# Starting the loads of queries and keys from ScalarE's DMA queue instead of SyncE's, from step 28 on

## The chip, the core and the metric

The kernel runs on one core of a Trainium2 chip. A core has a matrix engine (TensorE, PE in the profile, with its weight loads as PEld), three engines for everything else (VectorE or DVE, ScalarE or ACT, GpSimd or POOL), and SyncE (SP), which here only starts transfers. Transfers between the chip's main memory and the core's on-chip memory are done by 16 DMA engines. An engine starts one by an instruction in its own queue; an instruction that has to wait for a semaphore holds everything behind it in that queue. The metric is device time in microseconds (us).

## The reference

There are 8 batches, 8 heads, 512 local positions, 32 global positions and a head width of 64. Attention comes first, then a two-layer network with a SiLU-like gate on its output.

```python
k_all = concat([k_g, k_l]); v_all = concat([v_g, v_l])
out_g = softmax(q_g @ k_all.T / 8) @ v_all                # 32 global queries see everything
s_ll  = where(|i - j| <= 32, q_l @ k_l.T / 8, -1e9)       # a local query sees a band
out_l = softmax(concat([q_l @ k_g.T / 8, s_ll])) @ v_all  # and the global keys
x = concat([out_g, out_l]) as rows of 8 heads x 64 = 512  # 4608 rows
h = x @ w_in                                              # 512 -> 2048
out = (h * sigmoid(h)) @ w_out                            # 2048 -> 512
```

## The kernel before

**Attention** is cut into 128 steps: 8 batches by 4 chunks of 128 positions by 4 pairs of heads. A step `k` is made of parts, each a small function: `st_load` fetches queries and keys of the step (tile `raw`), `st_split` cuts them into a high and a low half (a cast on ScalarE, L345, and two subtractions on VectorE, L346 and L347, into the tiles `qk` and `klo`), `st_scores` does the score matmuls (L363, L364) and the softmax, `st_halves`, `st_away` and `st_back` transpose the probabilities by a copy on GpSimd (L393), a write to main memory (L398) and a transposing load (L402, tile `pt`), and `st_out` multiplies by the values (L444) for the four pairs of a chunk at once. Steps 0 to 27 have a shorter form: their `raw` (L323) is used as it is, without a split.

The **global queries** of a batch come in four loads (`g_load`, tile `raw_g`, L238), each with its own split (`g_split`: L247 on ScalarE, L248 and L249 on VectorE) and scores (`g_scores`). Those of batches 0 and 1 (`GF` = 2) are not split. Those of batch `b + 1` are placed among the steps of batch `b`; for batches 2 to 7 that is at every second step from the eighth on, so those of batch 2 begin at step 23.

The **network** runs over 12 blocks of three (the last two: two) tiles of 128 rows. A block is 16 units; a unit `f` is a first layer (12 matmuls, L600), a gate (tanh L607 on ScalarE, L608 on VectorE, the high half `gh` L610 on ScalarE, the low half `gl` L611 on VectorE) and a second layer (9 matmuls, L627). TensorE does the second layer of a unit after the first layer of the next one, so the gate has that long. The attention of the next block is woven into the units of this one: `put(when, part, ...)` gives each part a due time in steps, the parts are sorted by it, and `fill` and `advance` emit them between the matmuls as the units proceed.

**What sets the order.** TensorE keeps the order in which the program emits its instructions. The other engines' order is made by a planner from its estimate of all times, except that `hold(...)` pins an instruction behind the instruction emitted just before it for the same engine. All transfers of SyncE's queue are held, so that queue has program order: loads, writes of halves, transposing loads and values. A transposing load waits for the write of its halves and for TensorE to release a `pt` tile (there are four); the write waits for GpSimd's copy.

**The due times around the change.** A step's load is due 1.65 steps before its scores (`DMAT`), its split 0.5 before them. `SOONER` makes the loads of steps 9 to 15 due earlier. A `raw_g` load is due 0.9 before the place of its scores' step, its split 0.2 after it. From step 16 on, and for the global queries from batch 2 on, `raw` and `raw_g` share two buffers: a load waits until the split of the load two places before has read its buffer.

ScalarE's queue starts only the stores of the results (L645).

Of the kernel before, what the change touches and what calls it, by code (L numbers as in the profile page):

```python
# [32 lines left out]
GW = QG + SKV  # L33
# [6 lines left out]
BUFS = dict(qk=2, raw=2, p=2, halves=1, pt=4)  # L40
ND = 28
KF = 12
GF = 2
KP = 12
WHOLE, OWN, SOONER = 9, 7, -2.2
WARM = 288
WARMS = (14, 8, 1)
LEAN = 8
# [23 lines left out]
def attention_moe_kernel(ctx: ExitStack, tc: tile.TileContext, qk0_in, qk_in, v_in, gqk, wts, out):  # L72
    nc = tc.nc
# [15 lines left out]
    def attbank(kind, name):  # L89
        if early:  # L90
            i = next(banks[kind]) % {"s": 3, "t": 2, "o": 3}[kind]
            if i and kind == "s":
                return ps_h.tile([P, 512], F32, tag="h", name=name)
            if i:
                return ps_out.tile([P, 512], F32, tag="out2" if kind == "t" else f"out{i - 1}", name=name)
        else:
            kind = "sto"[next(banks["s"]) % 3]
        return ps_att.tile([P, 512], F32, tag=f"att{kind}", name=name)


    hold = tc.keep_in_program_order
# [66 lines left out]
    def raw_tile(name, whole=False):  # L168
        i = next(homes) if whole else 0
        if i > WHOLE + NPR - 1:  # L170
            return const.tile([P, 2 * DM], F32, tag=f"ws{12 - (i - WHOLE - NPR) % 6}", name=name)
        if whole and i == NPR:
            return scratch(13, F32, name)
        i = (i - (i > NPR)) % 4
        if i % 2 and 14 + i // 2 not in taken:
            return scratch(14 + i // 2, F32, name)
        return raws.tile([P, QW + KW], F32, tag="raw", name=name)
# [57 lines left out]

    def g_load(b, p):
        raw = raw_tile(f"raw_g{b}_{p}", b < GF)
        hold(nc.sync.dma_start(out=raw[:, :GW], in_=gqk[b, p]))  # L238
        state["graw", p] = raw

    def g_split(b, p):
        if b < GF:
            return
        raw = state.pop(("graw", p))
        hi, lo = qk_tiles(f"_g{b}_{p}")

        nc.scalar.copy(out=hi[:, QG : QG + GW], in_=raw[:, :GW])  # L247
        nc.vector.tensor_tensor(out=lo, in0=raw[:, QG:GW], in1=hi[:, 2 * QG : QG + GW].bitcast(F32), op=ALU.subtract)  # L248
        nc.vector.tensor_tensor(out=hi[:, :QG], in0=raw[:, :QG], in1=hi[:, QG : 2 * QG].bitcast(F32), op=ALU.subtract)  # L249
        state["gqk", p] = hi, lo  # L250

    def g_scores(b, p):
        did(("scores", b, p), *([("turn", b - 1, p // 2)] if b else []))
        rows = slice(QG * (p % 2), QG * (p % 2 + 1))
        if b < GF:
            raw = state.pop(("graw", p))
        else:
            hi, lo = state.pop(("gqk", p))
            both, kh = hi[:, : 2 * QG], hi[:, 2 * QG : GW + QG]
        if b < GF:  # L260
            s = attbank("so"[p % 2], f"gs{b}_{p}")
# [58 lines left out]
    def st_load(k, b, c, pr):  # L320
        raw = raw_tile(f"raw{k}", k < WHOLE + OWN)
        if k < ND:
            hold(nc.sync.dma_start(out=raw[:, : QW + W], in_=qk0_in[k]))  # L323
        else:
            hold(nc.sync.dma_start(out=raw, in_=qk_in[k - ND]))
        tiles["raw", k] = raw

    def st_vload(k, b, c, pr):
# [20 lines left out]
    def st_scores(k, b, c, pr):  # L349
# [28 lines left out]
        else:  # L378
            nc.scalar.activation(p[:, 0, :W], p[:, 0, :W], AF.Copy, scale=st[:, 6:7])  # L379
        if KF <= k < ND:  # L380
            nc.scalar.activation(p[:, 1, :W], p[:, 1, :W], AF.Copy, scale=st[:, 7:8])
# [23 lines left out]
    def st_turn(k, b, c, pr):  # L405
        if k < KF:
            t = attbank("t", f"t{k}")
            p = tiles.pop(("p", k))
            assert k in held_by.values()
            for i in range(4):  # L410
                nc.tensor.transpose(t[:, i * P : (i + 1) * P], p[:, i * P : (i + 1) * P], ident.bitcast(F32))
            pt = tiles["pt", k] = pt_tile(k)
            nc.scalar.copy(out=pt[:, :, :, :P], in_=t.rearrange("p (u a q) -> p u a q", u=2, a=2))
        else:
            pt = tiles["pt", k] = pt_tile(k)
        if k < NPR:
            return
        did(("last", b) if (c, pr) == (NC - 1, NPR - 1) else k, ("turn", b, pr // 2))
        pgt, pgu = state["pgt"]
        nc.gpsimd.tensor_copy(out=pt[:, :, 0, P:], in_=pgt[:, c, 2 * pr : 2 * pr + 2, :])  # L420
        if c == NC - 1:
            src = pgu[SG * pr : SG * (pr + 1), :].rearrange("p (u q) -> p u q", u=2)
            nc.gpsimd.tensor_copy(out=pt[:SG, :, 1, P:], in_=src)
# [75 lines left out]
    def put(when, fn, *a):  # L499
        stream.append((when, fn, a))  # L500

    AHEAD = NPR
    for k, (t, b, c, pr) in enumerate(steps):
        a = (k, b, c, pr)
        j = k % NST
        due = dict(DUE)
        if k >= KF:
            due.update(DMAT)
            due.update({} if pr else DMAT0)
        if WHOLE <= k < WHOLE + OWN:  # L510
            due["load"] = SOONER
        if k < AHEAD:
            due.update({part: FIRST[part][k] - k for part in ("load", "vload", "turn", "out")})
        elif pr == 0:
            due["vload"] = VLOADS[min(k // NPR, 3)]
        if k == AHEAD:
            for h in range(NPR):
                put(FIRST["gload"][h], g_load, 0, h)
                put(FIRST["gscores"][h], g_scores, 0, h)
            for hh in range(2):  # L520
                put(FIRST["gsoft"][hh], g_soft, 0, hh)
                put(FIRST["gturn"][hh], g_turn, 0, hh)
            put(FIRST["late"], g_late)
            at = FIRST["then"]
            for when in JOINS:
                put(at + when - NPR, join_weights)
            for f, when in enumerate(SPLITS):
                put(at + when - NPR, split_weights, f)
        if j == 0 and b:
            for hh in range(2):  # L530
                put(at + (TURN if b > 1 else TURN1)[hh], g_turn, b, hh)
        for f, half in FIRSTW.get(k, ()):
            put(at + 0.01, fetch_weights, f, half)
        put(at + due["load"], st_load, *a)
        put(at + due["split"], st_split, *a)
        put(at, st_scores, *a)
        if "vload" in due:
            put(at + due["vload"], st_vload, *a)
        if k >= KF:
            put(at + due["halves"], st_halves, *a)  # L540
            put(at + due["away"], st_away, *a)
        put(at + due["turn"], st_turn, *a)
        if k >= KF:
            put(at + due["back"], st_back, *a)
        if k < SINGLE or pr == NPR - 1:
            n = 1 if k < SINGLE else NPR
            put(at + due["out"], st_out, k - n + 1, n, b, c, t)
            marks[t] = at + due["out"]
        if j == NST - 1 and b % 4 == 3:
            put(marks[t] + 0.001, g_tile, t + 1)  # L550
            marks[t + 1] = marks[t] + 0.001
        if b + 1 < B:
            first, every = HEADS if b > 1 else HEADS0
            for h in [h for h in range(NPR) if first + h * every == j]:
                for part, fn in (("load", g_load), ("split", g_split), ("scores", g_scores)):
                    put(at + (SOONER if part == "load" and b + 1 < GF else HEAD[part]), fn, b + 1, h)
                if h % 2:
                    put(at + HEAD["soft"], g_soft, b + 1, h // 2)
                at += HEAD["slot"]
        at += 1.0  # L560
# [178 lines left out]
```

## Time and profile before

| | |
|---|---|
| time, median of 3 runs | 980.89 us (979.16 to 983.91) |
| the profiled execution | 978.29 us, span 976.5 us |
| TensorE busy | 949.8 us, 97% of the span |
| ScalarE busy | 580.5 us, 59% |
| VectorE busy | 626.5 us, 64% |
| loads `raw<-in_qk_dram` with a split | 100, of 352 KB, 3.4 us from issue to landing |
| loads `raw_g<-in_gqk_dram` | 32 (24 of them from batch 2 on), of 304 KB, 4.6 us |
| transposing loads `pt<-away` | 116, 3.3 us |

A row of the profile names a line of the kernel, the engine, the operation and `out<-in`. In a list of time, the first number is the start in us from the span's beginning and the second the duration; what stands in brackets is how long the engine had been idle before, and what ended it. `SPq` and `ACTq` are the queues in which SyncE and ScalarE start transfers; the time of such a row is that of starting it, not of the transfer. In a list of waits the three numbers are the sum in us, the count and the longest. The chain that ended last is followed back from the last instruction, each time to what released it.

### The profile page before, as it was taken

The page shows a single profiled execution, that of the slowest core. Times are in us where ns is not written, and L with a number is a line of the kernel's source. Part 1 is how long each engine was busy: PE and PEld are TensorE (multiplying, and loading weights), DVE is VectorE, ACT ScalarE, POOL GpSimd, SP SyncE. Part 2 cuts the span into 40 slices and gives each one's busy share as a digit, 9 for nine tenths or more (in the row PEclk, how much of TensorE's full clock was granted, in tenths as well). Part 3 has the DMA queues.
Part 4 walks back from the last instruction along what each step waited for, and adds up shares of the span by engine and source line. Part 5 has one row for each costly group of instructions (what it writes and reads, how often), then busy time and mean ns, then how long its engine had stood idle before and what let it go on. Part 6 is the DMA issues. An engine that isn't in the chain of part 4 may idle for free.

```text
span 976.5 us, 17412 instructions
## 1 busy us (share of the span) xinstructions
PE 949.8 (97%) x5774; PEld 848.3 (87%) x5774; DVE 626.5 (64%) x1893; ACT 580.5 (59%) x1486; POOL 201.4 (21%) x413
## 2 busy tenths in 40 slices
PE   8789999999999999999999999999999999999998
PEld 6579888998899989989899999989989899899897
DVE  5888977766666677656577567766677565453322
ACT  6878876665556656555566656666575665343332
POOL 2122232122221222112122222312222221120000
PEclk9999999999999999999999999999999999999999
DMA  9968967576565766534655676566665664433000
GB/s 302 392 194 210 280 160 205 151 168 173 147 167 155 198 153 179 166 93 110 187 158 159 147 213 173 144 193 153 167 186 152 161 163 141 121 90 87 1 22 22
DMA packets 189305, 157.32 MB, mean 161 GB/s; under 512 B 128672, under 2 KB 148640, under 8 KB 189216
## 3 DMA queue, kind: packets, MB, share of 16 engines
q1 hardware_dynamic: 184800, 148.28, 56.2%
q10 hardware_dynamic: 4416, 7.93, 2.3%
q8 instruction: 46, 0.75, 0.3%
q14 instruction: 43, 0.35, 0.1%
HBM read 86.44 MB, written 39.32 MB: 129 GB/s over the span
## 4 chain that ended last, share of the span: by engine, by line
PE 82%; ACT 6%; DVE 6%; DMA 4%; issue 1%; SPq 0%; ACTq 0%; POOL 0%; DVEq 0%
PE out L627 34%; PE h L600 34%; PE o L444 6%; DMA raw<-in_qk_dram 2%; PE s L363 2%; PE s L364 2%; DMA raw_g<-in_gqk_dram 2%; ACT probs L372 1%; PE s L361 1%; DVE w_lo L231 1%; DVE w L221 1%; PE gt L309 1%; DVE probs L368 1%; DVE gl L611 1%; PE gs L272 0%
## 5 line engine op out<-in xcount | busy, mean ns | idle before, releaser
L393 POOL COPY halves<-probs 128x512 uint16<-128x512 uint16 x232 | 152.7, 684 | 495.2 <-ACT probs L379 185.2
L607 ACT ACTIVATE t<-h 128x384 f32<-128x384 f32 (+1 forms) x192 | 90.6, 472 | 166.5 <-PE h L600 156.3
L608 DVE SCALAR_TENSOR_TENSOR t<-t,h 128x384 f32<-128x384 f32 (+1 forms) x192 | 101.6, 529 | 115.1 <-ACT t L607 114.3
L627 PE MATMUL out<-w_hi,gh 128*128 128x512 f32 x544 | 164.9, 402 | 3.0 <-ACT gh L610 2.9
L600 PE MATMUL h<-xh,w_hi 128*128 128x384 f32 (+1 forms) x768 | 161.1, 332 | 4.6 <-ACT w_hi L230 4.5
L627 PE MATMUL out<-w_hi,gl 128*128 128x512 f32 x544 | 162.0, 396 | 0.2 <-DVE gl L611 0.2
L627 PE MATMUL out<-w_lo,gh 128*128 128x512 f32 x544 | 161.7, 395 | 0.0
L600 PE MATMUL h<-xh,w_lo 128*128 128x384 f32 (+1 forms) x768 | 158.8, 328 | 0.1
L600 PE MATMUL h<-xl,w_hi 128*128 128x384 f32 (+1 forms) x768 | 158.8, 328 | 0.0
L372 ACT ACTIVATE probs<-probs,st 128x224 f32<-128x224 f32 x244 | 115.8, 475 | 60.4 <-DVE st L368 59.7
L600 PEld LDWEIGHTS h<-xh,w_hi 128*128 128x128 f32 x768 | 133.7, 189 | 19.8 <-ACT w_hi L230 6.3
L611 DVE TENSOR_TENSOR gl<-t,gh 128x384 fp32r<-128x384 f32 (+1 forms) x192 | 109.6, 571 | 43.5 <-ACT gh L610 39.1
L368 DVE CUSTOM_DVE_ANT_0 probs<-s,mask 128x224 f32<-128x224 f32 x244 | 85.8, 386 | 75.6 <-PE s L364 64.8
L600 PEld LDWEIGHTS h<-xl,w_hi 128*128 128x128 f32 x768 | 133.4, 189 | 0.0
L600 PEld LDWEIGHTS h<-xh,w_lo 128*128 128x128 f32 x768 | 131.8, 189 | 0.7 <-DVE w_lo L231 0.7
L610 ACT CAST gh<-t 128x384 fp32r<-128x384 f32 (+1 forms) x192 | 94.4, 492 | 53.5 <-DVE t L608 52.9
L627 PEld LDWEIGHTS out<-w_hi,gl 128*128 128x128 f32 x544 | 100.7, 189 | 23.1 <-DVE gl L611 1.3
L627 PEld LDWEIGHTS out<-w_lo,gh 128*128 128x128 f32 x544 | 100.7, 188 | 21.7 <-issue 0.6
L627 PEld LDWEIGHTS out<-w_hi,gh 128*128 128x128 f32 x544 | 93.6, 189 | 15.7 <-ACT gh L610 6.5
L345 ACT CAST qk<-raw 128x704 fp32r<-128x704 f32 x100 | 77.7, 777 | 28.3 <-DMA raw<-in_qk_dram 23.8
L346 DVE TENSOR_TENSOR klo<-raw,qk 128x448 fp32r<-128x448 f32 x100 | 65.3, 653 | 30.4 <-ACT qk L345 28.1
L379 ACT ACTIVATE probs<-probs,st 128x224 f32<-128x224 f32 x118 | 56.7, 481 | 32.4 <-DVE st L375 30.8
(95 smaller groups left out, 1066.0 us busy)
## 6 DMA issues: line engine op xcount, KB each, us to landing
raw<-in_qk_dram SPq DMA_DIRECT2D x100, 352.0 KB, 3.4
away<-halves SPq DMA_DIRECT2D x116, 256.0 KB, 2.7
vraw<-in_v_dram SPq DMA_DIRECT2D x30, 512.0 KB, 4.9
raw_w<-in_wts_dram SPq DMA_DIRECT2D x29, 512.0 KB, 6.7
raw_g<-in_gqk_dram SPq DMA_DIRECT2D x32, 304.0 KB, 4.6
out_dram<-o ACTq DMA_DIRECT2D x29, 256.0 KB, 3.6
raw<-in_qk_dram SPq DMA_DIRECT2D x28, 240.0 KB, 4.8
pt<-away SPq DMA_TRANSPOSE x116, 3.3
```

Source lines behind the costliest of these rows:

```text
L345: nc.scalar.copy(out=qk, in_=raw)
L346: nc.vector.tensor_tensor(out=klo[:, :KW], in0=raw[:, QW:], in1=qk[:, QW:].bitcast(F32), op=ALU.subtract)
L368: nc.vector.tensor_tensor_reduce(out=p[:, u, :W], in0=ss[u], in1=mask_of[c], scale=-SCALE, scalar=3.0e38, op0=ALU.add, op1=ALU.min, accum_ ...
L372: nc.scalar.activation(p[:, u, :W], p[:, u, :W], AF.Exp, bias=st[:, u : u + 1], scale=-1.0, accum_out=st[:, 2 + u : 3 + u])
L393: nc.gpsimd.tensor_copy(out=halves[:, :, u], in_=p[:, 2 * P * u : 2 * P * (u + 1)].bitcast(U16).rearrange("p (j h) -> p h j", h=2))
L444: nc.tensor.matmul(o[D * u : D * (u + 1), :m], vraw[:, a, u, :], pt[:, u, a, :m], start=(a == 0), stop=(a == 1))
L600: nc.tensor.matmul(h[:, :nt], wt[:, c * P : (c + 1) * P], x[:, c, :nt], start=(i == 0), stop=(i == 3 * NCC - 1))
L607: nc.scalar.activation(t[:, :nt], h[:, :nt], AF.Tanh, scale=0.5)
L608: nc.vector.scalar_tensor_tensor(out=t[:, :nt], in0=t[:, :nt], scalar=1.0, in1=h[:, :nt], op0=ALU.add, op1=ALU.mult)
L610: nc.scalar.copy(out=gh[:, :nt], in_=t[:, :nt])
L611: nc.vector.tensor_tensor(out=gl[:, :nt], in0=t[:, :nt], in1=gh[:, :nt].bitcast(F32), op=ALU.subtract)
L627: nc.tensor.matmul(outs[n][i], g[:, i * P : (i + 1) * P], w, start=(f == 0 and j == 0), stop=(f == NF - 1 and j == 2))
```

## The change

The loads of queries and keys from step 28 on (`OTHER`), which are the 100 loads with a split, and the 24 loads of global queries from batch 2 on are started from ScalarE's queue instead of SyncE's. They are still held, now behind the instruction that the program emitted just before for ScalarE. The due time of the step loads becomes 1.4 steps before the scores (`LATER`) instead of 1.65; that of the global loads stays.

```diff
 KF = 12
+OTHER = 28
 GF = 2
 KP = 12
-WHOLE, OWN, SOONER = 9, 7, -2.2
+WHOLE, OWN, SOONER, LATER = 9, 7, -2.2, -1.4
...
     def g_load(b, p):
         raw = raw_tile(f"raw_g{b}_{p}", b < GF)
-        hold(nc.sync.dma_start(out=raw[:, :GW], in_=gqk[b, p]))
+        hold((nc.scalar if b >= GF else nc.sync).dma_start(out=raw[:, :GW], in_=gqk[b, p]))
...
         else:
-            hold(nc.sync.dma_start(out=raw, in_=qk_in[k - ND]))
+            hold((nc.scalar if k >= OTHER else nc.sync).dma_start(out=raw, in_=qk_in[k - ND]))
...
             due.update(DMAT)
             due.update({} if pr else DMAT0)
+        if k >= OTHER:
+            due["load"] = LATER
```

## The prediction

> **What bounds the kernel now.** I read the page first, then the stretches of 25 us, then the chain that ended last, then SyncE's queue.
>
> ```profile
> span 976.5 us, 17412 instructions
> PE 949.8 (97%) x5774; PEld 848.3 (87%) x5774; DVE 626.5 (64%) x1893; ACT 580.5 (59%) x1486; POOL 201.4 (21%) x413
> ```
>
> TensorE is busy for 97% of the span, and its order and its work are the same after the change. So the change can only move what TensorE loses by waiting or by a lower clock. The change acts from step 23 (the first moved load of global queries) and step 28 on, which is from about 141 us. Where TensorE is not full after that:
>
> ```profile
> 150.00:875.00 725.00, 718.87 (x4333) 648.93 (x4333) 476.47 (x1426) 427.97 (x1081) 164.23 (x324) 1.00 0.60 158
> ```
> ```profile
> 150.00:175.00 25.00, 24.42 (x151) 21.77 (x151) 20.26 (x57) 16.46 (x41) 6.06 (x12) 1.00 0.66 186
> ...
> 225.00:250.00 25.00, 23.51 (x145) 21.24 (x145) 14.37 (x43) 13.61 (x34) 4.92 (x9) 1.00 0.70 195
> 250.00:275.00 25.00, 22.67 (x118) 20.17 (x115) 17.54 (x55) 15.58 (x40) 5.48 (x12) 0.93 0.59 160
> ...
> 350.00:375.00 25.00, 24.73 (x153) 22.07 (x152) 19.46 (x59) 16.41 (x41) 5.38 (x13) 1.00 0.73 182
> ...
> 450.00:475.00 25.00, 24.46 (x150) 21.83 (x148) 13.12 (x39) 11.60 (x30) 4.87 (x9) 1.00 0.43 121
> 475.00:500.00 25.00, 24.78 (x151) 22.06 (x152) 18.80 (x52) 16.66 (x40) 6.67 (x12) 1.00 0.62 164
> ...
> 625.00:650.00 25.00, 24.71 (x152) 22.04 (x151) 17.82 (x52) 15.71 (x40) 6.62 (x13) 1.00 0.59 172
> ...
> 825.00:850.00 25.00, 24.64 (x150) 21.93 (x150) 13.12 (x39) 11.67 (x30) 4.62 (x10) 1.00 0.39 103
> ```
>
> The first column is the length, the second TensorE's busy time; the last but two is the granted clock. From 150 to 875 us TensorE idles only 725.0 - 718.9 = 6.1 us, and all but 0.05 us of that lies in these eight stretches: 0.58, 1.49, 2.33, 0.27, 0.54, 0.22, 0.29 and 0.36 us. In the third one the clock was 0.93, which costs about 25 x 0.07 = 1.7 us more.
>
> So the **ceiling** of what a better start of loads can give in this stretch is 6.1 + 1.7 = 7.8 us, 0.8% of the time. (A rule of the Trainium skill bears on the 1.7: "TensorE: Matmul & The Clock Gate", Part 1, says that the clock falls after an idle window of about 3.4 us. By it a stall of 2.33 us need not cost any clock, and the ceiling would be 6.1 us. The row shows 0.93 behind such a stall; the measurement decides.)
>
> **Are these stalls late loads?** The chain that ended last, in order of time, goes through a load of queries and keys (raw) or of a global query (raw_g) ahead of nearly all of them:
>
> ```profile
> 158.94 0.42 DVE qk L347
> 159.39 4.34 DMA raw_g<-in_gqk_dram
> ...
> 231.15 4.85 DMA raw<-in_qk_dram
> ...
> 343.43 4.07 DMA raw<-in_qk_dram
> ...
> 468.34 5.40 DMA raw_g<-in_gqk_dram
> ...
> 635.18 0.04 ACT pg L274
> 635.22 5.33 DMA raw<-in_qk_dram
> ...
> 845.34 3.19 DMA raw<-in_qk_dram
> ```
>
> The stall at 254 us has no DMA piece in the chain, but stands behind a cast of a load that ScalarE took up after 2.48 us of idleness:
>
> ```profile
> 250.32 0.78 ACT L345 CAST qk<-raw 128x704 fp32r<-128x704 f32 x1 [2.48 <-PE o L444]
> ```
>
> The releaser named is the last by the profile, but TensorE was long in L444 then; the load that it casts started at 246.0 (below) and a landing takes 3.4 to 6.3 us (part 2). Why the loads start late shows on SyncE's queue:
>
> ```profile
> 224.36 0.36 SPq L238 DMA_DIRECT2D raw_g<-in_gqk_dram  x1
> 229.69 1.29 SPq L402 DMA_TRANSPOSE pt<-away  x1
> 231.15 0.46 SPq L325 DMA_DIRECT2D raw<-in_qk_dram  x1
> ...
> 244.63 1.23 SPq L402 DMA_TRANSPOSE pt<-away  x1
> 246.02 0.57 SPq L325 DMA_DIRECT2D raw<-in_qk_dram  x1
> ```
> ```profile
> SPq L402 <- DMA away<-halves: 188.3, 79, 5.0
> ...
> SPq L402 <- PE o L444: 110.3, 23, 10.0
> ...
> SPq L325 <- DVE qk_g L249: 9.4, 7, 1.9
> SPq L238 <- DVE qk_g L249: 4.3, 1, 4.3
> ```
>
> The queue stood from 224.7 to 229.7 us for a transpose (L402) and the load came behind it. In 150 to 900 us SyncE waits 188 us for its own writes of halves and 110 us for TensorE to release a pt buffer, up to 10 us at once, and each time the loads behind wait with it. The loads' own waits for a buffer are small: 9.4 + 4.3 = 13.7 us on VectorE in these rows.
>
> **The change, part by part.**
>
> 1. *Removed*: 100 loads (L325) and 24 loads (L238) no longer stand behind L402's and L398's waits. I go through the stalls. Those at 239, 254, 351, 475 (two stretches) and 850 us follow a load that stood behind a transpose or behind what a transpose held up: 1.49 + 2.33 + 0.27 + 0.54 + 0.22 + 0.36 = 5.2 us, with the clock 6.9 us. Two loads waited for their buffer and not for the queue: 159.39 came right behind the VectorE work that frees it (L347, to 159.36), 635.22 right after ScalarE's L274. Those stalls, 0.58 + 0.29 us, I leave standing. Bounds: nothing removed, or all 7.8 us.
>
> 2. *Added on ScalarE*: 124 issues. The trace has no load there, but it has output stores:
>
> ```profile
> L645 ACTq DMA_DIRECT2D out_dram<-o x33: 327/339/435, 229.5 to 973.1; - x33
> ```
> ```profile
> L325 SPq DMA_DIRECT2D raw<-in_qk_dram x100: 327/367/2200, 147.0 to 860.3; - x100
> ...
> DMA to landing us min/median/max: 2.9/3.4/6.3
> ```
> ```profile
> PEld out L627 <- ACT gh L610: 4.2, 11, 0.9
> ```
>
> At 0.34 us each (the row nearest to it, ScalarE's own) that is 42 us, and ScalarE is idle for 725.0 - 428.0 = 297 us of this stretch, so it fits. It reaches TensorE only where the second layer already waits for gh: 11 weight loads did. How many units of a first and a second layer there are in the stretch is the count of tanh (L607) in it:
>
> ```profile
> 150.00:875.00 725.00, 69.80 (x143) 1.00 0.60 158
> ```
>
> With 143 units of 725 / 143 = 5.1 us, issues that all met a waiting unit would cost 11 x 124 / 143 x 0.34 = 3.2 us. An issue hurts only if it falls between tanh and gh, some 2 of the 5.1 us (the chain of C below), so I take 0.4 of it, 1.3 us. Bounds: 0 and 3.2.
>
> 3. *Moved*: the load is due at -1.4 steps instead of -1.65, just behind the split of the step before (-0.5 - 1 = -1.5). From its first to its last load in the row above a step takes (860.3 - 147.0) / 99 = 7.2 us. So the load is 0.9 steps = 6.5 us ahead of its own cast on the same queue, against a landing of 3.4 us in the median and 6.3 at most: it lands in time if both keep their places. The buffer it needs is the one of two loads back, whose split lies 1.1 steps = 7.9 us behind, so its wait should be over. I take 0 for the move; it becomes a loss if the planner puts the cast nearer to the load (a rival, below).
>
> 4. *SyncE* loses 124 issues (124 x 0.37 = 46 us) and the 13.7 us of waits, so away and transposes start a little earlier. I take nothing: no wait of TensorE for pt stands behind 146 us. The loads now share the 16 DMA engines with the transposes rather than queue behind them; at a DMA share of 0.60 I count nothing.
>
> 5. *Before 150 us* only two global loads move. I count nothing; the bound is +-1.5 us, the size of the largest single stalls.
>
> **Sum**: -6.9 + 1.3 = -5.6 us. The profiled execution took 978.3 us (span 976.5 and 1.8 around it), so 972.7 us for the same execution. The median before, 980.89, lies 2.6 us above that, so I forecast 980.9 - 5.6 = 975.3 us.
>
> **The rivals.**
>
> *B, the cast follows too closely.* The planner orders ScalarE by its own estimate of when a load lands. If it draws the casts forward to some 3 us behind the load, ScalarE stands at each long landing (6.3 against 3 is 3.3 us), more often than today:
>
> ```profile
> ACT qk L345 <- DMA raw<-in_qk_dram: 23.8, 22, 2.5
> ```
>
> Today 22 such waits make the stalls of about 4 to 7 us. With as many left, the gain is 1 to 2 us: 979.5 us. For it: load and cast come nearer by 0.25 steps. Against: 6.5 us between them.
>
> *C, slower: ScalarE is held by a load's wait for its buffer.* The 13.7 us that SyncE waits for VectorE at these two lines would hold ScalarE and with it tanh and gh of the next unit. From the end of h to the need of gh lie one second and one first layer of 2.1 us each, less a chain of 0.47 + 0.53 + 0.49 us and the gaps between (some 0.3 us), about 2.4 us of slack; beyond that TensorE stops:
>
> ```profile
> 840.71 2.08 PE out L627 x9
> 842.79 2.09 PE h L600 x12
> ```
> ```profile
> L607 ACT ACTIVATE t<-h 128x384 f32<-128x384 f32 (+1 forms) x192 | 90.6, 472 | 166.5 <-PE h L600 156.3
> L608 DVE SCALAR_TENSOR_TENSOR t<-t,h 128x384 f32<-128x384 f32 (+1 forms) x192 | 101.6, 529 | 115.1 <-ACT t L607 114.3
> ...
> L610 ACT CAST gh<-t 128x384 fp32r<-128x384 f32 (+1 forms) x192 | 94.4, 492 | 53.5 <-DVE t L608 52.9
> ```
>
> The longest such wait today, 4.3 us, would cost 1.9 us and, like the stall at 254, 1.7 us of clock. Four of these are 14 us: 980.9 - 5.6 + 14 = 989 us; it is slower than before from two such holds on (7.2 us against 5.6). Against: the later due time makes these waits shorter.
>
> *D, the load doesn't start sooner.* If what holds a load is the moving of data and not SyncE's queue, time stays at 980.9. The Trainium skill says this in "DMA: Bandwidth & Descriptors", section "Issuing engines are not separate DMA queues": all queues run on the same 16 engines, and a second one saves only the time of starting, usually small. Against D stand the 110 us and 188 us of waits at L402, ahead of which a load cannot start; the page does not speak of waits.
>
> **How the numbers follow.** Forecast 0.50, B 0.24, C 0.16, D 0.10. A measurement of this kernel tells about 0.5% (4.9 us) from no change. The forecast is only 0.7 us beyond that, so a fifth of it falls within: faster 0.40, and 0.03 from B with a smaller loss, together 0.43. Slower: most of C, and little of B, 0.16. The rest, 0.41, is the same. The forecast's own range is 971 (all 7.8 us, from the lowest run 979.2) to 979; with the 1.5 us before 150 us the low end is 969.5, and B, D and the beginning of C put the high end at 984.
>
> **What would show it.** Right: no load in SyncE's queue after 145 us but vraw; TensorE's idle time from 150 to 875 us near 2 us instead of 6.1; no stretch with a clock of 0.93 there; ScalarE's waits at L345 for the load under 10 us; the chain without loads. Wrong by B: these waits at 20 us or more. Wrong by C: ScalarE's queue waiting at L238 or L325 for VectorE for over 2.4 us, followed by idle TensorE. Wrong by D: loads that start at the same times and land late.

## The result and the profile after

The changed kernel is slower: 992.1 us in the median (985.0 to 994.4), against 979.7 us before; the ratio is 1.012 with a 95% interval of 1.008 to 1.016. The profiled execution took 994.38 us, the longest of the six; its span is 992.3 us, 15.8 us more than before, where the medians lie 12.4 us apart. In the changed file the lines behind the new constant stand one lower and those behind the new due time three lower: the load is L326 there, its cast L346, the global load L239 and its cast L248, tanh L610, `gh` L613, the second layer L630.

The page of the changed kernel: span, the engines, and the chain that ended last.

```profile
span 992.3 us, 17361 instructions
...
PE 952.6 (96%) x5774; PEld 846.9 (85%) x5774; DVE 617.6 (62%) x1893; ACT 577.8 (58%) x1486; POOL 199.9 (20%) x413
...
PE 68%; DMA 12%; DVE 10%; ACT 7%; issue 2%; ACTq 0%; SPq 0%; DVEq 0%
PE h L603 29%; PE out L630 28%; DMA raw<-in_qk_dram 9%; PE o L445 5%; DMA raw_g<-in_gqk_dram 3%; ACT probs L373 2%; PE s L364 2%; PE s L365 2%; DVE t L611 1%; DVE w_lo L232 1%; DVE probs L369 1%; DVE gl L614 1%; ACT qk L346 1%; PE s L362 1%; DVE klo L347 1%
```

The loads, which were to leave the chain, hold 12% of it (9% and 3%); all transfers together held 4% before. The stretches (length, TensorE busy, ..., granted clock, DMA share, GB/s):

```profile
150.00:875.00 725.00, 705.57 (x4226) 633.40 (x4225) 460.26 (x1406) 419.74 (x1069) 158.80 (x317) 1.00 0.60 157
```
```profile
350.00:375.00 25.00, 19.94 (x117) 16.63 (x116) 14.70 (x44) 13.44 (x34) 5.60 (x11) 0.95 0.68 141
...
500.00:525.00 25.00, 23.14 (x145) 20.63 (x144) 16.59 (x51) 14.98 (x37) 5.44 (x13) 1.00 0.61 159
```

TensorE idles 725.0 - 705.6 = 19.4 us from 150 to 875 us, against 6.1 before: 13.3 us of the 15.8. It is no single accident: one stretch loses 5.1 us, several others 1 to 2.3.

What TensorE stood for longest between 150 and 900 us, first in the changed kernel, then in the kernel before (sum in us, times, longest):

```profile
PE gs L273 <- DVE acc L459: 6.5, 5, 3.5
PE out L630 <- ACT gh L613: 6.1, 6, 1.5
PE s L364 <- DVE qk L348: 5.9, 6, 1.9
```
```profile
PE gs L272 <- DVE acc L458: 2.3, 1, 2.3
PE s L363 <- DVE qk L347: 1.5, 1, 1.5
PE out L627 <- ACT gh L610: 1.5, 4, 0.5
```

The three rows differ by 4.2 us at the scores of global queries (`gs`; VectorE's `acc`, which reads the output of the attention, comes late), by 4.6 us at the second layer, which stood for the gate's `gh`, and by 4.4 us at the scores of the steps. So the loss reaches TensorE in three places, and only one of them is a wait for the step's own queries and keys.

ScalarE's waits for the loads in the changed kernel (sum in us, times, longest):

```profile
ACT qk L346 <- DMA raw<-in_qk_dram: 52.7, 39, 5.0
...
ACT qk_g L248 <- DMA raw_g<-in_gqk_dram: 25.8, 20, 5.1
```

Together 78.5 us at the two casts. Before it was 23.8 us at L345 and, in this row of the kernel before, 6.4 at L247, together 30.2 us:

```profile
ACT qk_g L247 <- DMA raw_g<-in_gqk_dram: 6.4, 7, 1.9
```

How one such wait comes about shows in ScalarE's queue of the changed kernel, step 72 and 73:

```profile
489.81 0.79 ACT L346 CAST qk<-raw 128x704 fp32r<-128x704 f32 x1
...
497.60 0.35 ACTq L326 DMA_DIRECT2D raw<-in_qk_dram  x1
...
498.35 0.48 ACT L380 ACTIVATE probs<-probs,st 128x224 f32<-128x224 f32 x1
498.37 0.35 ACTq L239 DMA_DIRECT2D raw_g<-in_gqk_dram  x1
501.65 0.78 ACT L346 CAST qk<-raw 128x704 fp32r<-128x704 f32 x1 [2.82 <-DMA raw<-in_qk_dram]
```

and what TensorE does then:

```profile
503.67 0.34 PE L364 MATMUL s<-qk 128*128 128x224 f32 x1 [1.86 <-DVE qk L348]
```

The load starts at 497.60, 7.8 us after the cast of the step before, behind softmax and gate instructions (and ScalarE's waits for their inputs), and only 6.1 us ahead of its own scores. Two instructions and the start of a global load later, ScalarE meets the cast of that same load and stands for 2.82 us until it lands. TensorE loses 1.86 us. SyncE's queue, in which the load stood before, was past a transpose at 491.5 and started nothing until 494.3; whether the load would have stood ahead of the write there is not shown:

```profile
490.21 1.29 SPq L403 DMA_TRANSPOSE pt<-away  x1
494.31 0.34 SPq L399 DMA_DIRECT2D away<-halves  x1
```

The worst one is a global load, in the chain of the changed kernel:

```profile
358.45 7.46 DMA raw_g<-in_gqk_dram
365.92 0.02 issue
365.94 0.02 ACT qk_g L248
365.97 0.04 issue
366.00 3.46 DMA raw<-in_qk_dram
```

It took 7.46 us to land, ScalarE stood 5.1 us for it, and the next load could not start before ScalarE was past that cast, at 366.00. The two landings come one behind the other because both loads and both casts share one queue. This is the stretch with 5.1 us of idleness and a clock of 0.95.

### The profile page after: what moved, and what is told of

Its sections match the earlier page's. It is cut to its first block, busy times and chain, and to the rows that moved or that the text cites. A ratio compares the mean times of both kernels' runs of the same rounds, so it can differ in the third digit from the quotient of the medians.

```text
span 992.3 us, 17361 instructions
## 1 busy us (share of the span) xinstructions
PE 952.6 (96%) x5774; PEld 846.9 (85%) x5774; DVE 617.6 (62%) x1893; ACT 577.8 (58%) x1486; POOL 199.9 (20%) x413
## 4 chain that ended last, share of the span: by engine, by line
PE 68%; DMA 12%; DVE 10%; ACT 7%; issue 2%; ACTq 0%; SPq 0%; DVEq 0%
PE h L603 29%; PE out L630 28%; DMA raw<-in_qk_dram 9%; PE o L445 5%; DMA raw_g<-in_gqk_dram 3%; ACT probs L373 2%; PE s L364 2%; PE s L365 2%; DVE t L611 1%; DVE w_lo L232 1%; DVE probs L369 1%; DVE gl L614 1%; ACT qk L346 1%; PE s L362 1%; DVE klo L347 1%
## 5 line engine op out<-in xcount | busy, mean ns | idle before, releaser
L610 ACT ACTIVATE t<-h 128x384 f32<-128x384 f32 (+1 forms) x192 | 90.2, 470 | 168.0 <-PE h L603 153.7
L630 PE MATMUL out<-w_hi,gh 128*128 128x512 f32 x544 | 165.6, 402 | 6.4 <-ACT gh L613 6.1
L630 PE MATMUL out<-w_hi,gl 128*128 128x512 f32 x544 | 161.9, 396 | 0.2 <-DVE gl L614 0.2
L630 PE MATMUL out<-w_lo,gh 128*128 128x512 f32 x544 | 161.1, 394 | 0.0
L613 ACT CAST gh<-t 128x384 fp32r<-128x384 f32 (+1 forms) x192 | 94.1, 490 | 48.9 <-DVE t L611 48.8
L630 PEld LDWEIGHTS out<-w_hi,gl 128*128 128x128 f32 x544 | 100.6, 189 | 22.8 <-DVE gl L614 1.2
L630 PEld LDWEIGHTS out<-w_lo,gh 128*128 128x128 f32 x544 | 100.5, 188 | 21.5 <-issue 0.6
L346 ACT CAST qk<-raw 128x704 fp32r<-128x704 f32 x100 | 78.1, 781 | 58.8 <-DMA raw<-in_qk_dram 52.7
L630 PEld LDWEIGHTS out<-w_hi,gh 128*128 128x128 f32 x544 | 93.4, 189 | 20.5 <-ACT gh L613 10.2
```

Source lines behind the costliest of these rows:

```text
L346: nc.scalar.copy(out=qk, in_=raw)
L610: nc.scalar.activation(t[:, :nt], h[:, :nt], AF.Tanh, scale=0.5)
L613: nc.scalar.copy(out=gh[:, :nt], in_=t[:, :nt])
L630: nc.tensor.matmul(outs[n][i], g[:, i * P : (i + 1) * P], w, start=(f == 0 and j == 0), stop=(f == NF - 1 and j == 2))
```

## The experiments

Three theories went in. N: in ScalarE's queue a cast stands too near behind its load, and ScalarE stands before it. L: the later due time is at fault, whatever the queue. Q, and later S: standing in ScalarE's queue costs by itself, through the work ahead of it or the start. A number read from the order alone, without any time, goes with them: how many other ScalarE instructions stand between a load and its cast. Counted in the trace of the changed kernel (without the starts of transfers and the reading of sums), that is 5 in the median for the step loads, for 37 of the 100 no more than 3; for 20 of the 24 global loads it is 1 or 2. In time, without ScalarE's wait itself: ScalarE came to 39 of the step casts and 19 of the global ones less than 3.5 us behind the start of their load, 3.5 us being the median landing of a step load; in the kernel before it did so at 18 and 1.

**The due time alone, on SyncE's queue.**

```diff
-        hold((nc.scalar if k >= OTHER else nc.sync).dma_start(out=raw, in_=qk_in[k - ND]))
+        hold(nc.sync.dma_start(out=raw, in_=qk_in[k - ND]))
```

The global loads are put back to SyncE in the same way; `LATER` stays.

> All loads stay on SyncE's queue; only the due time of the step loads goes from -1.65 to -1.4. Theory N (the cast is placed too near behind its load in ScalarE's queue, and ScalarE stands before it): the load is later by 0.25 steps, 1.8 us, on a queue that is often ahead, so ScalarE's waits for loads at the casts go from 30 to 35-45 us and the time to 980-984 us. Theory L (it is the later due time, whatever the queue): as slow as the changed kernel, 990-994 us, waits near 75 us. Theory Q (it is that the load stands in ScalarE's queue behind late ScalarE work): as before, 979-981 us.

Measured: 981.1 us, ratio 1.0024 (1.0008 to 1.0040), waits at the casts 34.1 + 6.2 us. L falls as the cause of the 1.2%; the due time alone, on SyncE's queue, costs 0.2%.

**The queue alone, with the old due time.**

```diff
-WHOLE, OWN, SOONER, LATER = 9, 7, -2.2, -1.4
+WHOLE, OWN, SOONER, LATER = 9, 7, -2.2, -1.65
```

> The changed kernel with the old due time of -1.65 for the step loads, now on ScalarE's queue. In the built program the cast then stands behind its load by 2 other ScalarE instructions in the median, against 5 in the changed kernel. Theory N: slower still, 996-1006 us, ScalarE's waits for loads at the casts over 100 us (78 in the changed kernel). Theory L: back to 980-984 us, since the loads are due as early as before. Theory Q: between, 985-992 us, since the load stands a quarter of a step earlier in the same queue.

Measured: 1019.8 us, ratio 1.043 (1.040 to 1.047). The waits of this kernel's ScalarE:

```profile
ACT qk L346 <- DMA raw<-in_qk_dram: 139.9, 75, 4.4
...
ACT qk_g L248 <- DMA raw_g<-in_gqk_dram: 31.3, 21, 2.6
```

171 us of waits; 75 of the 100 step casts stood. TensorE's longest wait is now the second layer's for the gate's `gh` (6.1 us in the changed kernel):

```profile
PE out L630 <- ACT gh L613: 17.1, 16, 2.8
```

An earlier due time made it slower, not faster; N had the direction, but not the size (996 to 1006 us were expected). So of the two things in the change, the later due time is what kept it from being 4% slower.

**Only the step loads, only the global loads.** The first keeps the change but for L239, which stays on SyncE; the second is the kernel before with L238 alone on ScalarE.

> The changed kernel, but the 24 global loads stay on SyncE's queue; the 100 step loads are on ScalarE's, due at -1.4, 5 other instructions ahead of their casts in the median as in the changed kernel. Theory N: the casts of global loads no longer stand 1 instruction behind their load, which takes away most of the 26 us of waits there and about a third of the loss: 985-989 us. Theory L: 990-994 us, since the due time of the step loads is the same. Theory Q: 989-992 us, a fifth of the loads less.

> The kernel before with only the 24 global loads on ScalarE's queue; the step loads stay on SyncE's with their due time of -1.65. In the built program the casts of the global loads stand 2 other ScalarE instructions behind their load in the median. Theory N (the cast stands too near behind its load in ScalarE's queue): waits at L247/L248 for the load go from 6 to 25-35 us, and the time to 982-987 us, which with the step loads' part (984.7 without the global ones) makes up the loss of the changed kernel. Rival S (each start costs ScalarE its 0.34 us, wherever the cast is): 24 of 124 starts, 980-981 us.

Measured: 984.7 us (ratio 1.0070, 1.0042 to 1.0098) with 54.3 + 8.2 us of waits, and 983.5 us (ratio 1.0073, 1.0041 to 1.0105) with 18.0 + 29.4 us. Each part costs about 0.7%, and each brings ScalarE's waits at its own cast. 24 global loads cost as much as 100 step loads; their casts stand nearer (2 instructions in the median against 5), but that this is why was not tested.

**The casts held.**

```diff
-        nc.scalar.copy(out=qk, in_=raw)
+        hold(nc.scalar.copy(out=qk, in_=raw))
...
-        nc.scalar.copy(out=hi[:, QG : QG + GW], in_=raw[:, :GW])
+        hold(nc.scalar.copy(out=hi[:, QG : QG + GW], in_=raw[:, :GW]))
```

> The changed kernel with one thing more: the casts of the loads (L346, L248) are held behind the instruction emitted just before them for ScalarE, so that the planner can't draw them forward. In the built program the cast then stands behind its load by at least 5 other ScalarE instructions, 7 in the median (1 and 5 without). Theory N: ScalarE's waits for loads at the casts fall from 78 to under 25 us and the time to 972-981 us. Theory L: 988-994 us, the loads start as late. Theory Q: 988-996 us, the loads stand behind the same ScalarE work, and casts come later.

Measured: 1063.5 us, ratio 1.088 (1.085 to 1.091). N's number fell. Its first half held: the list of ScalarE's waits has no load in it any more. But the cast now came too late for TensorE, which waited for it in person:

```profile
PE s L364 <- DVE qk L348: 57.7, 47, 3.0
```

So there are two distances, not one. From load to cast must be longer than a landing, and from cast to scores longer than the time by which ScalarE runs behind TensorE. The due times of the change leave 1.4 steps for both. In the traces the holds widen the first from 4.2 to 7.5 us in the median (up to ScalarE's arrival at the cast) and shrink the second from 8.5 to 2.1 us (up to TensorE's arrival at the scores).

**Room on both sides.** Loads due at -2.0, casts held and due at -1.0 (global -1.4 and -0.3). A relative has the loads as in the kernel before, on SyncE's queue at -1.65, and only the casts held and due at -1.0 (global -0.1).

> The changed kernel, all loads on ScalarE's queue, but with room on both sides of the cast: loads due at -2.0 steps (global ones -1.4), casts held behind the instruction emitted before them and due at -1.0 (global ones -0.3). Each cast then stands at least 4, in the median 7 to 8, instructions behind its load, as with the casts held alone, and half a step (3.6 us) earlier against its scores. Theory N with two sides (load to cast must be longer than the landing, cast to scores longer than ScalarE's lag; with the casts held alone the second failed, TensorE waited 58 us for qk): TensorE's waits for qk under 10 us, ScalarE's waits for loads under 20 us, time 973-983 us. Rival S (standing in ScalarE's queue is what costs): 990 us or more.

> The kernel before, all loads on SyncE's queue with their old due times, but the casts held and due at -1.0 (global ones -0.1). Nothing moves to ScalarE. If the planner's drawing forward of the casts is what makes ScalarE wait for loads also in the kernel before (30 us at the casts), these waits fall under 10 us and the time to 970-978 us. If they come from loads that start late behind the transposes, whatever the place of the cast, 977-983 us and the waits stay near 30 us.

Measured: 986.5 us (ratio 1.0082, 1.0058 to 1.0105) on ScalarE, 988.4 us (ratio 1.0108, 1.0084 to 1.0132) on SyncE. Both miss what N expected. ScalarE's waits for loads are gone (1.9 and 0.9 us), but TensorE still waits 10.6 and 14.7 us for `qk`: the casts still came too late. That the two queues are this near, with loads due differently, speaks against Q and S.

**What a start costs.** The kernel before with one more, tiny transfer on ScalarE's queue beside each of the 124 loads:

```diff
+        if k >= ND:
+            hold(nc.scalar.dma_start(out=junk, in_=qk_in[k - ND][:, :1]))
```

> The kernel before, with all loads on SyncE's queue, and beside each of the 124 loads one more transfer on ScalarE's queue, held there, of one column (4 bytes in each of 128 rows) into a tile that nobody reads: it prices the start on ScalarE alone. Theory N: 124 x 0.34 = 42 us of ScalarE's idle time, of which next to nothing reaches TensorE: 978-982 us. Rival S: 985 us or more, most of the loss of the changed kernel.

Measured: 983.2 us, ratio 1.0056 (1.0034 to 1.0078). But every one of them wrote the same tile, so a start waited for the transfer before it, and ScalarE with it; the three longest rows:

```profile
ACT gh L615 <- DMA junk<-in_gqk_dram: 7.5, 3, 3.1
ACT probs L377 <- DMA junk<-in_qk_dram: 6.9, 3, 4.5
ACT t L612 <- DMA junk<-in_qk_dram: 5.2, 3, 2.6
```

That prices the waits of starts, not the starts themselves. With 16 tiles in turn (`junk[next(nth) % 16]`):

> The price of a start on ScalarE again: as the issue-only kernel, but the 124 extra transfers go to 16 tiles in turn. With one tile each start waited for the transfer before it (20 us of ScalarE's waits for that tile), which is not what was to be priced. Theory N (the cast near its load is what costs): 977-981 us, within 0.3% of before. Rival S (the starts cost): 983 us or more, as the issue-only kernel.

Measured: 975.3 us, ratio 0.9994 (0.9973 to 1.0014). The start itself costs nothing that can be measured, and S falls.

**More room, on both queues.** Loads due at -2.4, casts held and due at -1.4, global ones at -1.8 and -0.7; a twin with the same due times has all loads on SyncE.

```diff
-WHOLE, OWN, SOONER, LATER = 9, 7, -2.2, -1.4
+WHOLE, OWN, SOONER, LATER = 9, 7, -2.2, -2.4
...
-DUE = dict(load=-1.2, split=-0.5, turn=1.6, out=2.2)
+DUE = dict(load=-1.2, split=-1.4, turn=1.6, out=2.2)
...
-HEAD = dict(load=-0.9, split=0.2, scores=0.8, soft=1.0, slot=0.3)
+HEAD = dict(load=-1.8, split=-0.7, scores=0.8, soft=1.0, slot=0.3)
```

> All loads on ScalarE's queue, casts held, as in the kernel with room on both sides, but all 0.4 steps (2.9 us) earlier: loads due at -2.4, casts at -1.4 (global ones -1.8 and -0.7). There TensorE still waited 11 us for qk and the margin between qk and the scores was 1.3 us in the median. Theory N with two sides: margin over 3 us, TensorE's waits for qk under 3 us, ScalarE's for loads under 10 us, time 970-979 us, below before. If held casts cost by themselves (they push other ScalarE and VectorE work behind them): 982-988 us.

> The same due times and held casts, with all loads on SyncE's queue. With room, ScalarE's queue against SyncE's made 0.26% less time (986.5 against 988.4). If the queue alone brings what the forecast said (the loads are free of the transposes' waits), this one is 3-8 us slower than its twin on ScalarE; if not, within 2 us of it.

Measured: 969.9 us, ratio 0.9932 (0.9909 to 0.9955), on ScalarE's queue; 974.6 us, ratio 0.9982 (0.9957 to 1.0008), on SyncE's. From 150 to 875 us, on ScalarE's queue

```profile
150.00:875.00 725.00, 723.92 (x4390) 656.46 (x4389) 485.99 (x1437) 434.03 (x1096) 171.91 (x327) 1.00 0.62 162
```

TensorE idles 1.1 us, and on SyncE's queue 4.3 us:

```profile
150.00:875.00 725.00, 720.70 (x4347) 652.92 (x4346) 484.29 (x1434) 430.80 (x1089) 168.82 (x328) 1.00 0.63 161
```

With room, ScalarE's queue is 4.7 us faster in the medians; the two intervals against the kernel before just don't meet. That is as much as was expected if the forecast's reason were right, but the trace doesn't show that reason. SyncE's 4.3 us are nearly all one wait, at 174 us, and not for a load of queries and keys but for a transposing load:

```profile
PE o L445 <- DMA pt<-away: 4.1, 1, 4.1
```

From 175 to 875 us TensorE doesn't idle on SyncE's queue either, although every load there still stands among the transposes. The profiled execution took 979.7 us, 5.1 us above the median of its kernel, so the one wait can't be taken for the 4.7 us. What they come from stays open.

**The same due times without the holds.**

> The kernel with early loads and casts on ScalarE's queue (loads at -2.4, casts at -1.4, global ones -1.8 and -0.7), without the holds: the planner may draw the casts forward again. In the built program the casts of step loads stand 7 instructions behind their load in the median as with the holds, those of global loads 4 instead of 9; 26 of 124 casts stand fewer than 4 behind (with the holds 3). If room by the due times is enough, as fast as with the holds: 968-972 us and under 10 us of ScalarE's waits for loads. If the holds are needed, 974-980 us and waits of 20 us or more, most of them at the global loads' casts.

Measured: 969.7 us, ratio 0.9914 (0.9889 to 0.9939). ScalarE's waits:

```profile
ACT qk L346 <- DMA raw<-in_qk_dram: 12.8, 11, 2.4
ACT qk_g L248 <- DMA raw_g<-in_gqk_dram: 3.0, 3, 1.5
```

15.8 us of waits, between the two expectations, but as fast as with the holds. Due times with room are enough; the holds are not needed. This is the change under study with four due times moved (load and cast, of the steps and of the global queries), and it beats both kernels. The same four due times on SyncE's queue without the holds were not run, so the two queues are compared at these due times only with holds.

The waits and the time, all with the loads moved in whole or in part or with another due time and without holds:

| kernel | ScalarE's waits for loads, us | time against before |
|---|---|---|
| before | 30.2 | 1 |
| SyncE, due -1.4 | 40.3 | 1.0024 |
| only global loads on ScalarE | 47.4 | 1.0073 |
| only step loads on ScalarE | 62.5 | 1.0070 |
| the change | 78.5 | 1.0120 |
| ScalarE, due -1.65 | 171.2 | 1.0433 |
| ScalarE, due -2.4, casts -1.4 | 15.8 | 0.9914 |

## Why the prediction was wrong

**The bound and the ceiling** were right. TensorE's order is the same, its stalls from 150 to 875 us are what moved, and with room they fell from 6.1 to 1.1 us (1.6 without the holds). In time the best version gains 0.9%, about the ceiling of 7.8 us, or 0.8%.

**Part 1, what is removed (-6.9 us)**, took for granted that a load which no longer stands behind SyncE's waits starts sooner. It exchanged one queue in program order for another. ScalarE's queue carries the gate and the softmax and waits for TensorE: the prediction's own row of L607 has 156.3 us of waits for `h`, which hold a load behind them as SyncE's waits do, and no term counts them. In the traces the load of a step started 12.8 us before its scores in the median, against 13.2 in the kernel before and 11.8 with the same due time on SyncE's queue; but 11 of the 100 loads started less than 7 us before them, against 2 and 3. So the gain didn't come, and no run shows the term: with early due times TensorE's stalls behind loads went away on either queue, and the 4.7 us between the twins have no such stall behind them in the traces.

**Part 2, the starts (+1.3 us)**, was small and can't be told from none (0.9994, 0.9973 to 1.0014; 1.3 us would be 1.0013). The duration was right, as the first row of the changed kernel shows; the second has the load's own waits for a semaphore, in ns:

```profile
L326 ACTq DMA_DIRECT2D raw<-in_qk_dram x100: 334/334/1272, 145.9 to 870.5; - x100
L326 ACTq EVENT_SEMAPHORE  x27: 17/17/1159, 145.3 to 793.0; - x27
...
DMA to landing us min/median/max: 2.8/3.5/7.1
```

**Part 3, the move (taken as 0)**, is the step that failed. It set 6.5 us between load and cast against a landing of 3.4 us, "if both keep their places". They did not: the planner drew the casts forward, to 5 instructions behind a step load in the median and 1 behind a global one. ScalarE came to them 4.2 and 2.5 us behind the start of the load instead of 6.5, and with landings of 3.5 us in the median and 7.1 at most it stood 78.5 us there instead of 30.2. TensorE's idle time rose from 6.1 to 19.4 us.

The distance had been taken from the due times alone; in the trace of the kernel before it is 4.9 us in the median, at a due distance of 8.3 (1.15 steps). The global loads, which make a third of the 78.5 us, have no distance in this part at all. And the 6.5 us were only one of two distances; the other, from cast to scores, was never worked out. The room for the buffer was not what was worked out either: where a global load lies between two step loads, the split two places back is due only 0.1 steps ahead of the load, not 1.1. That did little harm here, since the longest wait of a step load for a semaphore was 1.16 us (the row above).

**The rivals.** B named this mechanism, with "ScalarE's waits at L345 of 20 us or more" as its sign, and the sign came (52.7 us). Its price had the wrong sign: it held the waits to be as many as before and left a gain, where they grew to 2.6 times as much. That put the loss outside the range.

C, the rival for slower, had the path but not the cause. A standing ScalarE does hold tanh and `gh` of the next unit: a third of TensorE's loss is there, and ahead of the four longest of these stalls (at 211, 297, 354 and 660 us) ScalarE had stood 2 to 5 us at the casts. But it stood there for a landing. A load's own wait for its buffer, which C named, was never longer than 1.16 us, and C needs 2.4. B's cause on C's path is what was not priced.

D fell as well, since the time moved: the same loads at the same due time of -1.65 gave 4.3% more time on ScalarE's queue, and at -2.4, with the casts held, 0.5% less. The rule cited from the Trainium skill ("DMA: Bandwidth & Descriptors", "Issuing engines are not separate DMA queues"), that a second queue saves only the time of starting, is therefore not the whole price here; it speaks of what is saved and not of waits. Step loads landed in 3.5 us in the median, against 3.4 before, so the moving of data did not change. What changed is what a load stands behind and what stands behind it.

**The 0.93 clock** behind a long stall has its like in the changed kernel (0.95 in the stretch with 5.1 us of idleness, 3.51 us of it at once), so pricing a stall above its length was right. It doesn't follow each time: in the kernel with the old due time on ScalarE's queue, a stall of 2.51 us at 735 us left the clock of its stretch at 1.00.

## What to carry to other kernels

A transfer that an engine starts and also consumes has three places in one queue, the start, the consumer and whoever waits for the result, and both gaps must be long enough: start to consumer longer than the landing, consumer to user longer than that engine's lag. Moving the start alone to another queue changes both; move the due times with it, and count how many instructions stand between start and consumer before trusting the distance in time. Where a planner places the consumer, the due time moves it but doesn't fix it, and an engine's idle share says nothing about this.

## What had not been expected of the hardware

124 starts of tiny transfers on ScalarE cost nothing that these runs can measure (0.9994, 0.9973 to 1.0014), while 124 starts that may have to wait for the transfer before them cost 0.56%: what costs is the wait in an in-order queue. Landings of the same 304 KB load spread widely from ScalarE's queue too, up to 7.46 us in the case shown, against a median of 3.4. What stays open is why the planner spreads loads and casts better at -2.4 and -1.4 (7 instructions between them, without holds) than at -1.65 and -0.5 (2): the order was read, its cause was not looked into.
